# Making the low part of a narrowed weight piece on VectorE instead of GpSimd

## The chip, the core and the metric

The kernel runs on one core of a Trainium2 chip. The metric is device time in microseconds (us), the median of several executions. Five engines work side by side, each through its own instructions in program order: TensorE (PE in the rows, with its weight loads as PEld), VectorE (DVE), ScalarE (ACT), GpSimd (POOL) and SyncE (SP), which here only issues transfers. They wait for one another by semaphores.

## What is computed

Clustered attention, then a mixture of experts with one expert for a token, then a bilinear layer. Only the last two matter here:

```python
def _moe_ref(x, expert_emb, tau, w1, w2):
    ...
    for e in range(E):
        mask = expert_idx == e
        h = np.maximum(x[mask] @ w1[e], 0.0)
        out[mask] = gate_w[mask, None] * (h @ w2[e])

def _moe2_ref(x, w_a, w_b, w_out):
    a = x @ w_a
    b = x @ w_b
    return (a * b @ w_out).astype(np.float32)
```

There are 1536 tokens of 512 features, 8 experts with 1024 hidden features, and 1536 features in the bilinear layer. `w_a`, `w_b` and `w_out` come as 64-bit floats; the other weights as 32-bit ones.

## The kernel before

**Two-part numbers.** TensorE multiplies numbers of a rounded 32-bit type (fp32r). Each operand is therefore held as a high part (the value rounded to that type) and a low part (the value less the high part), and each product is three matmuls: high by high, low by high and high by low.

**Stages.** After attention come 64 expert steps (8 experts of 8 steps, G = 0 to 63) and 72 bilinear steps (I = 0 to 71, G = 64 on). In an expert step, `layer1` makes 12 matmuls of 256 columns; ScalarE takes the high part of the result (`hh`, L944), VectorE the low part (`hl`, L945). `layer2` multiplies what was made two steps before (LAG = 2), with 6 matmuls of 512 columns. In a bilinear step, `bil1` makes 24 matmuls of 256 columns into `ab`; ScalarE copies the first half to `ga` (L1005), VectorE multiplies by the second half (L1006), ScalarE rounds to `gh` (L1009) and VectorE makes `gl` (L1013). `bil2`, two steps later, makes 6 matmuls of 512 columns with `gh` and `gl`. The bank that a step's matmuls write is that of two steps before: TensorE can't start a step until VectorE has read that bank (`hl` or `ga`). At G = 53, G = 61 and I = 1, eight transposes on TensorE and two VectorE instructions of 128x512 (`xTl`, L869) prepare the rows of the next expert or block, and at G = 57 and I = 1 a copy `ys` of 128x512 (L967) is added on VectorE.

**Narrowing.** The 64-bit weights are 36 pieces of 128x512 numbers, 4 in a chunk and 9 chunks. A piece comes by a transfer of 512 KB into one of four `raw` buffers. ScalarE (`narrow_a`, L823) makes `a`, the absolute value taken from the upper words; VectorE (`narrow_b`, L835 to L837) puts in the low bits and the sign, in three instructions, in place. A step later ScalarE (`narrow_c`, L843) copies `a` to the chunk's high part `hi`, and GpSimd (L844) makes the low part, `a` less `hi`. `raw` is free again after L837, `a` (five buffers) after L844. An expert step narrows one piece, from G = 53 on; an even bilinear step one, an odd one two, until the 36 are done at I = 16. The lists `narrowed` and `late` hand pieces from one function to the next; from I = 2 on an even bilinear step finds two pieces in `late`, an odd one one.

**Order.** No scheduler moves instructions: each engine runs what the Python loop writes, in that order. In a bilinear step VectorE has `ga`, the three of one piece, `gl` and, in an odd step, the three of a second piece. In an expert step it has `hl` and then the three of one piece. Chunks 3 and 4 are first read at I = 8, chunks 6 and 7 at I = 16.

Of the kernel before, what the change touches and what calls it, by code (L numbers as in the profile page):

```python
# [44 lines left out]
def kernel(  # L45
# [15 lines left out]
    nc = tc.nc  # L61
# [667 lines left out]
    def result_rows():  # L729

        GA = [P, B * NT, NE]
        GB = B * NT
        tmp = big.tile([P, DM], F32, tag="a", name="rr", bufs=NA)
        t3 = tmp[:, :GB * NE].rearrange("p (t e) -> p t e", e=NE)
        t1, t2, t4, slot_f = (tmp[:, GB * (NE + i):GB * (NE + i + 1)] for i in range(4))
        nc.vector.tensor_copy(slot_f, slot_i)
        for dst, val in ((t1, ebase), (t2, pbase.rearrange("p (o e) -> p o e", o=1)), (t4, obase.rearrange("p (o e) -> p o e", o=1))):
            nc.vector.tensor_tensor(out=t3, in0=oh_all, in1=val.to_broadcast(GA), op=ALU.mult)
            nc.vector.tensor_reduce(out=dst, in_=t3, axis=AX.X, op=ALU.add)

        nc.vector.tensor_sub(slot_f, slot_f, t1)
        nc.vector.tensor_scalar(out=t1, in0=slot_f, scalar1=float(CAP), scalar2=None, op0=ALU.is_ge)
        nc.vector.tensor_sub(t4, t4, t2)
        nc.vector.scalar_tensor_tensor(out=t4, in0=t4, scalar=-float(CAP), in1=t1, op0=ALU.add, op1=ALU.mult)
        nc.vector.tensor_add(t4, t4, t2)
        nc.vector.tensor_add(slot_f, slot_f, t4)
        nc.vector.tensor_copy(slot_i, slot_f)
# [34 lines left out]

    narrowed = []
    late = []

    def open_part():
        n, j = divmod(nsplit[0], 4)
        if j == 0:
            hl[n] = big.tile([P, 2, 4, 512], F32R, tag=f"w{n % NSLOT}", name=f"w_{n}")
        w = raw.pop(nsplit[0])  # L790
        nsplit[0] += 1
        return w, hl[n][:, 0, j, :], hl[n][:, 1, j, :]
# [17 lines left out]
    def split_some(m):  # L810
        for _ in range(m):
            split_hi(1)
            split_lo()
# [3 lines left out]
    def narrow_a(m):  # L817
        for _ in range(min(m, 4 * NCH - nsplit[0])):
            load_raw()
            w, hi, lo = open_part()  # L820
            if w.dtype == I32:
                a = big.tile([P, 512], F32, tag="a", name=f"a_{nsplit[0]}", bufs=NA)
                nc.scalar.activation(a, w[:, :, 1].bitcast(F32), AF.Abs, scale=2.0 ** -112)  # L823
                narrowed.append((w, a, hi, lo))
            else:
                nc.scalar.copy(hi, w)
                nc.gpsimd.tensor_sub(lo, w, hi)
            ndone[0] += 1
            load_raw()

    def narrow_b(m):
        for _ in range(min(m, len(narrowed))):
            w, a, hi, lo = narrowed.pop(0)
            low, top, au = w[:, :, 0].bitcast(U32), w[:, :, 1].bitcast(U32), a.bitcast(U32)
            nc.vector.tensor_scalar(out=au, in0=au, scalar1=3, scalar2=None, op0=ALU.logical_shift_left)  # L835
            nc.vector.scalar_tensor_tensor(out=au, in0=low, scalar=29, in1=au, op0=ALU.logical_shift_right, op1=ALU.bitwise_or)  # L836
            nc.vector.scalar_tensor_tensor(out=au, in0=top, scalar=0x80000000, in1=au, op0=ALU.bitwise_and, op1=ALU.bitwise_or)  # L837
            late.append((a, hi, lo))

    def narrow_c():  # L840
        while late:
            a, hi, lo = late.pop(0)
            nc.scalar.copy(hi, a)  # L843
            nc.gpsimd.tensor_sub(lo, a, hi)  # L844


    xe_t = {}
# [10 lines left out]
    def trans_x(key, src, first=False):  # L858

        hi = big.tile([P, DC, CAP], F32R, tag="xTh", name=f"xTh_{key}", bufs=2)  # L860
        lo = big.tile([P, DC, CAP], F32R, tag="xTl", name=f"xTl_{key}", bufs=2)
        pts = [ps_t.tile([P, 2, CAP], F32, tag=("pp", "pv")[u], name=f"xT_{key}_{u}") for u in range(2)]
        for t in range(CT):
            for j in range(DC):
                nc.tensor.transpose(pts[j // 2][:, j % 2, t * P:(t + 1) * P], src[:, t, j * P:(j + 1) * P], ident)
        for u in range(2):
            (nc.vector.tensor_copy if u and first else nc.scalar.copy)(hi[:, 2 * u:2 * u + 2, :], pts[u])
        for u in range(2):
            nc.vector.tensor_sub(lo[:, 2 * u:2 * u + 2, :], pts[u], hi[:, 2 * u:2 * u + 2, :])  # L869
        xT_t[key] = (hi, lo)  # L870

    def mm3(ps, pairs):

        ops = [o for (sh, sl_), (mh, ml) in pairs for o in ((sh, mh), (sl_, mh))]
        ops += [(sh, ml) for (sh, _), (_, ml) in pairs]
        for i, (s_, m_) in enumerate(ops):
            nc.tensor.matmul(ps, s_, m_, start=(i == 0), stop=(i == len(ops) - 1))  # L877
# [57 lines left out]
    def layer1(G):  # L935
        e, f = divmod(G, NF)
        c, ff = divmod(f, 4)
        w = hl[4 * e + 2 * c]
        xh, xl = xT_t[e]
        ph = ps_t.tile([P, CAP], F32, tag=f"et{G % 2}", name=f"h_{G}")  # L940
        mm3(ph, [((w[:, 0, j, ff * P:(ff + 1) * P], w[:, 1, j, ff * P:(ff + 1) * P]), (xh[:, j, :], xl[:, j, :])) for j in range(DC)])
        hh = big.tile([P, CAP], F32R, tag="hh", name=f"hh_{G}", bufs=4)
        hlo = big.tile([P, CAP], F32R, tag="hl", name=f"hl_{G}", bufs=4)
        nc.scalar.activation(hh, ph, AF.Relu)  # L944
        nc.vector.scalar_tensor_tensor(out=hlo, in0=ph, scalar=0.0, in1=hh, op0=ALU.max, op1=ALU.subtract)  # L945
        hs[G] = (hh, hlo)
# [48 lines left out]
    def bil1(I):  # L995
        ck, f = order[I]
        c, ff = divmod(f, 4)
        xh, xl = xT_t["b", ck]
        pab = ps_t.tile([P, 2, CAP], F32, tag=f"et{I % 2}", name=f"ab_{I}")
        for z in range(2):  # L1000
            w = hl[NCE + 3 * c + z]
            mm3(pab[:, z, :], [((w[:, 0, j, ff * P:(ff + 1) * P], w[:, 1, j, ff * P:(ff + 1) * P]), (xh[:, j, :], xl[:, j, :])) for j in range(DC)])
        narrow_a(PACE[I % len(PACE)] > 0 if I >= I0 else 0)
        ga = big.tile([P, CAP], F32, tag="ga", name=f"ga_{I}", bufs=2)
        nc.scalar.copy(ga, pab[:, 0, :])  # L1005
        nc.vector.tensor_mul(ga, pab[:, 1, :], ga)  # L1006
        gh = big.tile([P, CAP], F32R, tag="hh", name=f"gh_{I}", bufs=4)
        gl = big.tile([P, CAP], F32R, tag="hl", name=f"gl_{I}", bufs=4)
        nc.scalar.copy(gh, ga)  # L1009
        narrow_c()  # L1010
        narrow_a(PACE[I % len(PACE)] > 1 if I >= I0 else 0)
        narrow_b(1)
        nc.vector.tensor_sub(gl, ga, gh)  # L1013
        narrow_b(1)
        gs_[I] = (gh, gl)

    def bil2(I):
# [36 lines left out]
    for G in range(total_f + tot + LAG):  # L1054
        I = G - total_f

        room = 4 * (NSLOT + 2 * (max(G - LAG, 0) // 4)) - nsplit[0]
        if 4 * NCE <= nsplit[0] and I < 0:
            narrow_a(min(room, 1))
        if I < 0:  # L1060
            layer1(G)
            e, f = divmod(G, NF)
            if G == 2 * NF:
                result_rows()
            if G > 3 * NF:
                next(gg, None)
            if f == 5:
                if e + 1 < NE:
                    trans_x(e + 1, xe_t[e + 1])
                else:  # L1070
                    trans_x(("b", 0), x2_t[0])
                if e + 2 < NE:
                    load_xe(e + 2)
                else:
                    load_x2(e + 2 - NE)
        elif I < tot:
            bil1(I)
            ck, f = order[I]
            if I == 1:
                trans_x(("b", 1), x2_t[1])  # L1080
            if I == X2:
                load_x2(2)
                load_x2(3)
            if ck > 0 and f == NF2 - 2 and ck + 1 < NCK:
                trans_x(("b", ck + 1), x2_t[ck + 1])
                if ck + 3 < NCK:
                    load_x2(ck + 3)
        if G - LAG >= total_f:
            bil2(I - LAG)
        elif G >= LAG:  # L1090
            layer2(G - LAG)
        put_rows(G - LAG)
        if nsplit[0] < 4 * NCE:
            split_some(min(room, 2 * G + lead - nsplit[0], RAMP0 + RAMP * G - nsplit[0], 4 * NCE - nsplit[0]))
        elif I < 0:
            narrow_c()
            narrow_b(1)


# [28 lines left out]
```

## Time and profile before

| | |
|---|---|
| median of 3 executions | 836.23 us (835.68 to 838.9) |
| the profiled execution | 841.22 us, its span 839.5 us |
| expert steps | up to 509 us of the span |
| the 36 pieces are narrowed | 478 to 602 us |
| bilinear steps | from 509 us |

The profile is one execution. Its page gives the busy time of every engine over the whole span; the trace behind it can be asked for a stretch, a line, or for instructions in order of time. A time in brackets behind a row is idle time ahead of that instruction, with what ended it. The length given for an instruction overlaps the start of the next one; what an instruction costs in a row of others is the distance from its start to the next start, called its pitch below.

### The profile page before, as it was taken

Reading aid. Unit: us, or ns where it says so; the run is one execution under the profiler, and the core shown is the slowest. Engines: PE = TensorE matmul, PEld = TensorE weight load, DVE = VectorE, ACT = ScalarE, POOL = GpSimd, SP = SyncE. Lnnn points to the kernel's source line nnn. Section 1 sums busy time; section 2 is a strip of 40 time slices with the busy share of each in tenths; the row PEclk is TensorE's granted clock in tenths of the full one; section 3 lists DMA queues with packets and bytes.
Section 4 is the critical chain, followed back from the end, with each engine's and each line's share of the span. In section 5 each row is a group of like instructions: output and inputs, shape, how many; then the busy total and the mean of one; then the engine's idle time right before and its main releaser. Section 6 shows DMA issues by size and latency. Waiting matters only on the chain.

```text
span 839.5 us, 13963 instructions
## 1 busy us (share of the span) xinstructions
PE 794.1 (95%) x5362; PEld 671.9 (80%) x5362; DVE 497.8 (59%) x939; ACT 389.8 (46%) x848; POOL 188.9 (23%) x190
## 2 busy tenths in 40 slices
PE   8889999999999959899999999989999999999996
PEld 5667777677776639789999879878899999999996
DVE  6776676776777667695655499999622221222221
ACT  4555756657556546565555455445322221222211
POOL 5022203134000042232135354444311010010101
PEclk9999999999999979999999999999999999999999
DMA  6137223153120039776777756655010010000000
GB/s 190 39 98 244 57 59 93 40 179 111 29 58 11 1 110 313 266 234 248 250 209 215 194 179 218 213 169 162 14 51 26 9 44 1 1 26 1 27 1 25
DMA packets 45516, 92.63 MB, mean 110 GB/s; under 512 B 6392, under 2 KB 15224, under 8 KB 45440
## 3 DMA queue, kind: packets, MB, share of 16 engines
q1 hardware_dynamic: 41232, 81.67, 32.2%
q0 software_dynamic: 2304, 6.31, 2.0%
q10 hardware_dynamic: 1904, 3.67, 1.3%
q8 instruction: 44, 0.72, 0.4%
q14 instruction: 32, 0.26, 0.1%
HBM read 69.27 MB, written 14.69 MB: 100 GB/s over the span
## 4 chain that ended last, share of the span: by engine, by line
PE 37%; issue 33%; DVE 17%; DMA 6%; POOL 3%; ACT 3%; SPq 0%; POOLq 0%; ACTq 0%; DVEq 0%
PE et L478 7%; PE h L877 6%; PE pv L505 6%; PE y L960 5%; DMA raw<-in_moe_w_dram 5%; PE sc L449 3%; PE sc L450 3%; DVE a L836 3%; DVE nmx L458 2%; PE t L341 2%; DVE a L835 2%; DVE a L837 2%; DVE gl L1013 1%; PE st L366 1%; PE px L519 1%
## 5 line engine op out<-in xcount | busy, mean ns | idle before, releaser
L1006 DVE TENSOR_TENSOR ga<-ab,ga 128x256 f32<-128x256 f32 x72 | 30.4, 422 | 150.4 <-ACT ga L1005 150.4
L463 ACT ACTIVATE E<-sc,nmx 128x768 f32<-128x768 f32 x96 | 86.8, 904 | 64.9 <-DVE nmx L458 57.6
L458 DVE TENSOR_REDUCE nmx<-sc 128x1 f32<-128x768 f32 x96 | 91.6, 955 | 11.0 <-PE sc L450 9.1
L1005 ACT COPY ga<-ab 128x256 f32<-128x256 f32 x72 | 26.6, 370 | 152.9 <-PE ab L877 152.9
L478 PEld LDWEIGHTS et<-ident,E 128*128 128x128 f32 x576 | 63.1, 143 | 34.5 <-issue 12.9
L1032 PE MATMUL o<-w,gh 128*128 128x512 f32 x288 | 90.7, 396 | 0.0
L484 DVE COPY ET<-et 128x384 f32<-128x384 f32 x96 | 52.8, 550 | 62.3 <-PE et L478 62.1
L478 PE MATMUL et<-ident,E 128*128 128x128 f32 x576 | 83.8, 281 | 3.9 <-ACT E L463 3.6
L800 ACT CAST w<-raw 128x512 fp32r<-128x512 f32 x128 | 72.9, 619 | 25.1 <-DMA raw<-in_moe_w_dram 21.5
L806 DVE TENSOR_TENSOR w<-raw,w 128x512 fp32r<-128x512 f32 x96 | 70.5, 762 | 22.6 <-ACT w L800 16.8
L877 PEld LDWEIGHTS h<-xTh,w 128*128 128x128 f32 x512 | 68.8, 190 | 16.3 <-DVE hl L945 11.1
L960 PE MATMUL y<-w,hh 128*128 128x512 f32 x256 | 81.1, 398 | 0.0
L877 PE MATMUL h<-xTh,w 128*128 128x256 f32 x512 | 73.0, 285 | 7.0 <-DVE hl L945 6.2
L505 PE MATMUL pv<-ET,v 128*64 128x384 f32 (+2 forms) x408 | 73.2, 479 | 0.7 <-ACT ET L482 0.6
L449 PE MATMUL sc<-K,Q 80*128 80x512 f32 x192 | 73.2, 382 | 0.4 <-DMA Q<-ohT 0.4
L844 POOL TENSOR_TENSOR w<-a,w 128x512 fp32r<-128x512 f32 x36 | 55.5, 1551 | 72.8 <-ACT w L843 54.4
L806 POOL TENSOR_TENSOR w<-raw,w 128x512 fp32r<-128x512 f32 x32 | 42.9, 1340 | 111.0 <-ACT w L800 96.4
L1009 ACT CAST gh<-ga 128x256 fp32r<-128x256 f32 x72 | 29.2, 406 | 71.9 <-DVE ga L1006 71.9
L450 PE MATMUL sc<-K,Q 128*128 128x512 f32 x192 | 62.1, 344 | 0.0
L1043 POOL DMA_INDIRECT out_dram<-ot,res x12 | 11.7, 972 | 219.9 <-DVE ot L1042 218.6
L1032 PE MATMUL o<-w,gl 128*128 128x512 f32 x144 | 56.6, 393 | 2.3 <-DVE gl L1013 2.3
L1013 DVE TENSOR_TENSOR gl<-ga,gh 128x256 fp32r<-128x256 f32 x72 | 41.4, 574 | 25.9 <-ACT gh L1009 25.9
(268 smaller groups left out, 1595.1 us busy)
## 6 DMA issues: line engine op xcount, KB each, us to landing
raw<-in_moe_w_dram SPq DMA_DIRECT2D x64, 512.0 KB
raw<-in_moe_w_a_dram SPq DMA_DIRECT2D x12, 512.0 KB
raw<-in_moe_w_b_dram SPq DMA_DIRECT2D x12, 512.0 KB
raw<-in_moe_w_out_dram SPq DMA_DIRECT2D x12, 512.0 KB
xs_d<-zero SPq DMA_DIRECT2D x8, 512.0 KB
ys_d<-ys SPq DMA_DIRECT2D x16, 256.0 KB
xe<-xs_d ACTq DMA_DIRECT2D x7, 512.0 KB
v<-in_v_dram SPq DMA_DIRECT2D x8, 384.0 KB
```

Source lines behind the costliest of these rows:

```text
L449: nc.tensor.matmul(ps[:, lo:hi], Q3[:, qs], K3[:, h * S + lo:h * S + hi], start=True, stop=False)
L450: nc.tensor.matmul(ps[:, lo:hi], Q2[:, qs], K2[:, h * S + lo:h * S + hi], start=False, stop=True)
L458: nc.vector.tensor_reduce(out=nmx[pp][:, h, t:t + 1], in_=sc[s], axis=AX.X, op=ALU.max, negate=True)
L463: nc.scalar.activation(e, sc.pop(s), AF.Exp, bias=nmx[pp][:, h, t:t + 1], accum_out=sums[pp][:, t, h:h + 1])
L478: nc.tensor.transpose(pt[:, j * P:(j + 1) * P], e[:, kt * P:(kt + 1) * P], ident)
L505: nc.tensor.matmul(pv[h * D:(h + 1) * D, :], vt[:, h, kt, :], ets[g, h][:, kt, :n * P], start=(kt == 0), stop=(kt == NT - 1))
L800: nc.scalar.copy(hi, w)
L806: eng.tensor_sub(lo, w, hi)
L844: nc.gpsimd.tensor_sub(lo, a, hi)
L877: nc.tensor.matmul(ps, s_, m_, start=(i == 0), stop=(i == len(ops) - 1))
L960: nc.tensor.matmul(ys_ps[e][t], s_[:, t * P:(t + 1) * P], w[:, m_, ff, :], start=(f == 0 and i == 0), stop=(f == NF - 1 and i == 2))
L1032: nc.tensor.matmul(o_ps[ck][t], s_[:, t * P:(t + 1) * P], w_[:, m_], start=(f == 0 and i == 0), stop=(f == NF2 - 1 and j == len(o_f[ck]) - ...
```

## The change

`narrow_c` no longer makes the low part on GpSimd. It puts the piece into a new list `lows`, and a new function `narrow_d` makes the low parts on VectorE. It is called at the end of an expert step, after `narrow_b`, and at the end of `bil1`, after the last `narrow_b`.

```diff
+    lows = []
...
         while late:
             a, hi, lo = late.pop(0)
             nc.scalar.copy(hi, a)
-            nc.gpsimd.tensor_sub(lo, a, hi)
+            lows.append((a, hi, lo))
+
+    def narrow_d():
+        while lows:
+            a, hi, lo = lows.pop(0)
+            nc.vector.tensor_sub(lo, a, hi)
...
         narrow_b(1)
         nc.vector.tensor_sub(gl, ga, gh)
         narrow_b(1)
+        narrow_d()
         gs_[I] = (gh, gl)
...
         elif I < 0:
             narrow_c()
             narrow_b(1)
+            narrow_d()
```

VectorE's instructions before, in expert step G = 56 and at the start of the next: `a_...` is a piece, `hl_...` the low part of the step's result; the number behind a name is the buffer's.

```order
L945 SCALAR_TENSOR_TENSOR hl_6478<-h_6464,hh_6477 128x256
L835 TENSOR_SCALAR a_6460<-a_6460 128x512
L836 SCALAR_TENSOR_TENSOR a_6460<-raw_6345,a_6460 128x512
L837 SCALAR_TENSOR_TENSOR a_6460<-raw_6345,a_6460 128x512
L945 SCALAR_TENSOR_TENSOR hl_6511<-h_6497,hh_6510 128x256
```

The same place in the changed kernel, where later lines have moved down by 1 to 7; `w_...` is a chunk.

```order
L951 SCALAR_TENSOR_TENSOR hl_6478<-h_6464,hh_6477 128x256
L836 TENSOR_SCALAR a_6460<-a_6460 128x512
L837 SCALAR_TENSOR_TENSOR a_6460<-raw_6345,a_6460 128x512
L838 SCALAR_TENSOR_TENSOR a_6460<-raw_6345,a_6460 128x512
L850 TENSOR_TENSOR w_6347<-a_6428,w_6347 128x512
L951 SCALAR_TENSOR_TENSOR hl_6511<-h_6497,hh_6510 128x256
```

One instruction of 128x512 has come in ahead of the next step's `hl`; it works on the piece of the step before.

VectorE's instructions before, in bilinear steps 5 and 6 (an odd one and an even one), from the odd step's `ga` on:

```order
L1006 TENSOR_TENSOR ga_7076<-ab_7047,ga_7076 128x256
L835 TENSOR_SCALAR a_7072<-a_7072 128x512
L836 SCALAR_TENSOR_TENSOR a_7072<-raw_6915,a_7072 128x512
L837 SCALAR_TENSOR_TENSOR a_7072<-raw_6915,a_7072 128x512
L1013 TENSOR_TENSOR gl_7080<-ga_7076,gh_7079 128x256
L835 TENSOR_SCALAR a_7084<-a_7084 128x512
L836 SCALAR_TENSOR_TENSOR a_7084<-raw_6966,a_7084 128x512
L837 SCALAR_TENSOR_TENSOR a_7084<-raw_6966,a_7084 128x512
L1006 TENSOR_TENSOR ga_7131<-ab_7101,ga_7131 128x256
```

The changed kernel from the second piece of that odd step to the start of the next odd step (its buffer numbers differ by one from some row on):

```order
L836 TENSOR_SCALAR a_7083<-a_7083 128x512
L837 SCALAR_TENSOR_TENSOR a_7083<-raw_6966,a_7083 128x512
L838 SCALAR_TENSOR_TENSOR a_7083<-raw_6966,a_7083 128x512
L850 TENSOR_TENSOR w_6975<-a_7019,w_6975 128x512
L1012 TENSOR_TENSOR ga_7131<-ab_7101,ga_7131 128x256
L836 TENSOR_SCALAR a_7127<-a_7127 128x512
L837 SCALAR_TENSOR_TENSOR a_7127<-raw_6978,a_7127 128x512
L838 SCALAR_TENSOR_TENSOR a_7127<-raw_6978,a_7127 128x512
L1019 TENSOR_TENSOR gl_7135<-ga_7131,gh_7134 128x256
L850 TENSOR_TENSOR w_6975<-a_7072,w_6975 128x512
L850 TENSOR_TENSOR w_6975<-a_7083,w_6975 128x512
L1012 TENSOR_TENSOR ga_7182<-ab_7153,ga_7182 128x256
```

An odd step ends with one low part, an even step with two, each ahead of the next step's `ga`. VectorE has 36 instructions more than before, all of this kind. GpSimd has none left between the last rows of the expert weights and the first rows of the output.

## Rows read from the trace of the kernel before

**Rows 1.** The page, part 1: busy us, share of the span, instructions.

```profile
PE 794.1 (95%) x5362; PEld 671.9 (80%) x5362; DVE 497.8 (59%) x939; ACT 389.8 (46%) x848; POOL 188.9 (23%) x190
```

**Rows 2.** Windows: stretch, length, busy us (instructions) of each engine, granted clock, DMA, GB/s.

```profile
479.30:599.80 120.50, 112.32 (x744) 99.00 (x744) 117.21 (x162) 57.72 (x124) 54.19 (x35) 1.00 0.57 174
604.90:820.00 215.10, 215.10 (x1526) 202.43 (x1525) 50.55 (x112) 45.94 (x112) 10.62 (x20) 1.00 0.05 18
```

**Rows 3.** VectorE's groups by line, 479.3 to 599.8 us: count, busy us, mean ns, idle before.

```profile
L837 DVE SCALAR_TENSOR_TENSOR a<-raw,a 128x512 uint32<-128x512 uint32 x36 | 45.9, 1274 | 1.2
L836 DVE SCALAR_TENSOR_TENSOR a<-raw,a 128x512 uint32<-128x512 uint32 x36 | 26.0, 722 | 1.2
L1013 DVE TENSOR_TENSOR gl<-ga,gh 128x256 fp32r<-128x256 f32 x17 | 17.9, 1054 | 0.0
L835 DVE TENSOR_SCALAR a<-a 128x512 uint32<-128x512 uint32 x36 | 17.2, 477 | 0.0
```

**Rows 4.** Timeline (start us, length us) of VectorE and GpSimd, 508 to 512 us.

```profile
508.34 0.69 DVE L837 SCALAR_TENSOR_TENSOR a<-raw,a 128x512 uint32<-128x512 uint32 x1
508.95 0.42 DVE L945 SCALAR_TENSOR_TENSOR hl<-h,hh 128x256 fp32r<-128x256 f32 x1
509.28 0.42 DVE L835 TENSOR_SCALAR a<-a 128x512 uint32<-128x512 uint32 x1
509.73 0.69 DVE L836 SCALAR_TENSOR_TENSOR a<-raw,a 128x512 uint32<-128x512 uint32 x1
509.81 1.77 POOL L844 TENSOR_TENSOR w<-a,w 128x512 fp32r<-128x512 f32 x1 [2.52 <-issue]
510.46 1.67 DVE L837 SCALAR_TENSOR_TENSOR a<-raw,a 128x512 uint32<-128x512 uint32 x1
512.05 0.41 DVE L945 SCALAR_TENSOR_TENSOR hl<-h,hh 128x256 fp32r<-128x256 f32 x1
```

**Rows 5.** Timeline of VectorE: two low parts of expert weights (L806) in a row.

```profile
429.72 1.28 DVE L806 TENSOR_TENSOR w<-raw,w 128x512 fp32r<-128x512 f32 x2
```

**Rows 6.** The page, part 5: all low parts of expert weights on VectorE.

```profile
L806 DVE TENSOR_TENSOR w<-raw,w 128x512 fp32r<-128x512 f32 x96 | 70.5, 762 | 22.6 <-ACT w L800 16.8
```

**Rows 7.** Timeline of TensorE: where steps start, two transposes' rows, one wait.

```profile
479.84 1.21 PE L877 MATMUL h<-xTh,w 128*128 128x256 f32 x8 [0.67 <-DVE hl L945]
...
500.99 0.38 PE L865 MATMUL xT_('b', 0)_0_6663<-ident,x 128*128 128x128 f32 x2
...
501.78 0.71 PE L960 MATMUL y<-w,hh 128*128 128x512 f32 x2
...
503.26 1.12 PE L877 MATMUL h<-xTh,w 128*128 128x256 f32 x8
...
506.08 1.11 PE L877 MATMUL h<-xTh,w 128*128 128x256 f32 x8
...
549.99 0.39 PE L877 MATMUL ab<-xTh_('b', 0)_6661,w 128*128 128x256 f32 x1 [1.17 <-POOL w L844]
...
605.15 1.12 PE L877 MATMUL ab<-xTh_('b', 1)_6850,w 128*128 128x256 f32 x8
...
609.41 1.12 PE L877 MATMUL ab<-xTh_('b', 1)_6850,w 128*128 128x256 f32 x8
```

**Rows 8.** Timeline of VectorE in bilinear steps 5 to 7.

```profile
540.17 0.41 DVE L1006 TENSOR_TENSOR ga<-ab,ga 128x256 f32<-128x256 f32 x1
...
543.39 0.41 DVE L1013 TENSOR_TENSOR gl<-ga,gh 128x256 fp32r<-128x256 f32 x1
...
545.51 0.42 DVE L1006 TENSOR_TENSOR ga<-ab,ga 128x256 f32<-128x256 f32 x1
...
550.14 0.41 DVE L1006 TENSOR_TENSOR ga<-ab,ga 128x256 f32<-128x256 f32 x1
```

**Rows 9.** Timeline of ScalarE in bilinear step 6: the high parts of two pieces.

```profile
546.28 1.14 ACT L843 CAST w<-a 128x512 fp32r<-128x512 f32 x2
```

**Rows 10.** Waits of the queue that issues transfers, 455 to 606 us: total us, times, longest.

```profile
SPq L128 <- DVE a L837: 81.7, 29, 5.0
```

## The prediction

> **What bounds the kernel now.** I read the page first, then the windows of the stretch in which pieces are narrowed, then VectorE's groups there, then the timelines. The page says that TensorE is busy 95% of the span and VectorE 59% [rows 1]; that is a mean over unlike stages. From 479.3 to 599.8 us VectorE is busy 117.21 of 120.50 us and TensorE 112.32, while after 604.9 us TensorE is busy all 215.10 of 215.10 us [rows 2]. So the stretch is VectorE's, and adding anything to VectorE looks like a loss. What matters is what VectorE's time is made of.
>
> It is partly waiting in disguise. L837 takes 0.69 us when GpSimd is idle, and 1.67 us when GpSimd's low part runs beside it: GpSimd started at 509.81 and ended at 511.58, and L837, started at 510.46, ended 0.55 us after that [rows 4]. An undisturbed L837 holds the engine for 0.61 us (508.34 to 508.95), so it did its work behind GpSimd, not beside it. The page of the groups shows how much of this there is: undisturbed, L837 and L836 take 0.69 us, L835 0.42 and `gl` 0.41 [rows 4, 8]. 36 x 0.69 is 24.8 us against 45.9 for L837 and 26.0 for L836; 17 x 0.41 is 7.0 against 17.9 for `gl`; 36 x 0.42 is 15.1 against 17.2 for L835 [rows 3]. The excess is 21.1 + 1.2 + 10.9 + 2.1 = 35.3 us, or 0.98 us a piece. Behind each stretched instruction stands, in VectorE's order, the next `hl`, `ga` or `gl`, for which TensorE waits.
>
> **What TensorE could do.** An expert step without a wait is 503.26 to 506.08, 2.82 us; a bilinear one 605.15 to 609.41, 4.26 us; eight transposes take 500.99 to 501.78, 0.79 us [rows 7]. Between 479.84 and 605.15 lie 9 expert steps (G = 55 to 63), 20 bilinear ones (I = 0 to 19) and two sets of transposes: 9 x 2.82 + 20 x 4.26 + 2 x 0.79 = 112.16 us, while the trace has 125.31. So 13.15 us is the most that any change to VectorE or GpSimd can give here.
>
> **The change, part by part.** Removed: 36 instructions on GpSimd. GpSimd has nothing else in this stretch, so nothing moves up behind them; what goes is the 35.3 us that they put into VectorE's instructions.
>
> Added: 36 low parts on VectorE. The same shape, types and operation stands in L806, where two in a row took 1.28 us [rows 5]; less 0.69 for the last one (an undisturbed L837, of the same size [rows 4]) the pitch is 0.60, rounded up. The mean of all 96 there is 0.762 us, disturbed ones among them [rows 6]. I take 0.60, since GpSimd will be idle; 0.60 and 0.762 are the ends, and an end below nothing is excluded because the instruction occupies VectorE in any case. The sum on VectorE is 36 x 0.60 = 21.6 us more and 35.3 less.
>
> By step, with pitches of 0.33 for `hl`, 0.45 + 0.73 + 0.61 = 1.79 for the three of a piece [rows 4] and 0.33 for `ga` and `gl`, which have `hl`'s length: an expert step on VectorE is 3.10 us now (508.95 to 512.05 [rows 4]) and becomes 0.33 + 1.79 + 0.60 = 2.72, under TensorE's 2.82. Two bilinear steps are 9.97 us now (540.17 to 550.14 [rows 8]). They become 0.33 + 1.79 + 0.33 + 1.20 = 3.65 for the even one and 0.33 + 1.79 + 0.33 + 1.79 + 0.60 = 4.84 for the odd one: 8.49, against TensorE's 8.52. It is close, but VectorE may lag: by the order, TensorE needs `ga` of step I only at the start of step I + 2, which is two `bil2` and one `bil1` later, more than 4.26 us after the matmuls that `ga` reads.
>
> What stays: at G = 53, two `xTl` of (an estimate, from L806's pitch) 0.60 each stand ahead of the first piece, so that step takes VectorE 0.33 + 1.20 + 1.79 = 3.32, 0.5 us over TensorE; at G = 57 the copy `ys`, of that size too, makes 2.72 + 0.60 = 3.32, of which the three shorter steps ahead pay 0.3. I leave 0.8 us for these. `xTl` and `ys` at I = 1 fall into VectorE's lag. The gain is 13.15 - 0.8, about 12.3 us.
>
> The new waits. A low part waits for its high part, at the head of VectorE's queue, with the next `ga` or `hl` behind it. In bilinear step 6 both high parts are done at 547.42 [rows 9], 1.91 us after `ga` began at 545.51 [rows 8]; in the new order the first low part comes up 0.33 + 1.79 + 0.33 = 2.45 us after `ga` began. So it has 0.54 us in hand. Matmuls now wait for low parts of VectorE where they waited for GpSimd: at 549.99 TensorE got the last low part of the second chunk after 1.17 us of waiting [rows 7]. That part was done 549.99 - 545.51 = 4.48 us after `ga` of step 6 began, and will be 3.65 us after it, earlier in the step. `a` is freed with the low part, so no later either. The raw transfers follow VectorE by themselves: SyncE's queue spent 81.7 us waiting for L837, which frees their buffers [rows 10], and ScalarE and the transfers have their old order.
>
> A rule speaks against all this. Perfetto Trace Analysis of the Trainium skill (Optimizing Scalar/DVE Operations) says that with a saturated VectorE it may make sense to give work to ScalarE or even GpSimd; by it the low parts should stay where they are. The same paragraph warns that the two share a port to the memory, and SBUF — State Buffer (SBUF: two separate sides) makes that a lock under which the loser stands still for the whole instruction. The row at 510.46 bears out the second [rows 4]; the first alone would give the sum of the second rival below.
>
> **The rivals.**
> - *VectorE stays the bound.* A low part costs 0.762 and not 0.60, or the lows wait a little. Two bilinear steps are then 8.49 + 3 x 0.16 = 8.97, 0.45 over TensorE, eight times: 3.6 us; an expert step is 2.88, 0.06 over, ten times: 0.6. The gain is 12.3 - 4.2 = 8.1 us at the least. For it: the margin in a pair is only 0.03 us. Against it: L806's pitch, and the lag that is allowed.
> - *The stall isn't GpSimd's.* If something else in the stretch stretched VectorE's instructions, a transfer into the buffers say, the 35.3 us stay and 21.6 us come on top of an engine that has no room: 841.22 + 21.6, slower by 21.6 us. It decides from the point where more than 35.3 - 21.6 = 13.7 us, 0.38 a piece, stays. Against it: the end of L837 follows GpSimd's by 0.55 us, its own work.
> - *Low parts wait for ScalarE.* If the high parts come later by more than the 0.54 us in hand, VectorE's queue stops in every step. Some 27 steps have a low part; at 12.3 / 27 = 0.46 us each, so 1.0 us later, the gain is gone and the time is as before. ScalarE is busy 57.72 of 120.50 us [rows 2], which speaks against it.
> - *The change doesn't do what it says.* The order shows 36 more on VectorE and none left on GpSimd; I give this nothing.
>
> **How the numbers follow.** About 0.5% is what a measurement here tells from no change: 4.2 us. The forecast, a gain of 12.3 us, has 0.65; VectorE as the bound, a gain of 4.2 to 10, 0.22; no change, with ScalarE or a wait that I don't see, 0.07; slower, mostly the stall that isn't GpSimd's, 0.06. Faster is 0.65 + 0.22 = 0.87. The profiled execution would go from 841.22 to 828.9; the median of 836.23 lies 4.99 below that execution, and I take the gain from it: 823.9 us. The low end is all of the 13.15 us and the spread of a median, some 1.2 us on top: 821.9. The high end is the first rival's 836.23 - 8.1 = 828.1 with two of it for more waits: 830.1. The rest, under 0.2, lies above.
>
> **What would show it.** L837 at 0.69 us in all 36 places and `gl` at 0.41; the low part on VectorE at 0.69 with a pitch of 0.60; expert steps of 2.82 and pairs of bilinear steps of 8.5 on TensorE, without waits for `ga`, `gl` or the weights; VectorE busy for some 106 us in the stretch. The prediction is wrong if L837 stays long without GpSimd, if idle time stands ahead of the low parts on VectorE, with ScalarE's copy ending it, or if TensorE's step is above 2.82 or 4.26 with a wait for a raw transfer in front of ScalarE.

## The result, and the profile after

The changed kernel takes 829.85 us (median of four runs, 828.8 to 832.04); the kernel before takes 837.57 us (four runs, 835.68 to 841.27, three of them those that the prediction started from). The ratio is 0.9882, with a 95% interval of 0.9855 to 0.9909: faster by 1.2%. That lies within the stated range (821.9 to 830.1 us), close to its upper end, and 6 us above the forecast of 823.9.

The profiled executions are 841.22 us before and 830.12 after, 11.1 us apart. TensorE's start of step G = 55 and its start of bilinear step I = 20 enclose the stretch that the prediction speaks of. It was 125.31 us long (479.84 to 605.15 [rows 7]) and is now 113.30 (481.07 to 594.37): 12.01 us gained, where 12.3 was forecast. The difference to the 11.1 lies outside the stretch. The stretch begins 1.23 us later, after the same instructions as before (in two further executions of the changed kernel it begins at 478.83 and at 483.03, so this is spread between executions); what follows it is 0.32 us shorter.

The page, part 1 (busy us, share of the span, instructions), answers to [rows 1], and the window below it (length, then busy us and instructions of TensorE, its weight load, VectorE, ScalarE and GpSimd, granted clock, DMA share, GB/s) to [rows 2], both of the changed kernel:

```profile
PE 793.2 (96%) x5362; PEld 675.4 (82%) x5362; DVE 484.2 (58%) x975; ACT 390.9 (47%) x848; POOL 133.3 (16%) x154
```

```profile
479.30:599.80 120.50, 119.61 (x824) 110.66 (x823) 107.03 (x205) 63.34 (x133) 0.00 (x0) 1.00 0.55 176
```

VectorE does 36 instructions more and is busy 13.6 us less over the span. In the window it falls from 117.21 to 107.03 us, while it gets through 205 instructions where it had 162 (in the stretch itself, 481.07 to 594.37, it is busy 105.33 of 113.30 us); GpSimd has none left there; TensorE is busy 119.61 of 120.50 us. The bound has passed from VectorE to TensorE.

VectorE's groups by line in the same window of the changed kernel (count, busy us, mean ns, idle us before) answer to [rows 3]. Later lines have moved down: L837 of before is L838 now, L836 is L837, L835 is L836 and L1013 is L1019; L850 is the low part.

```profile
L837 DVE SCALAR_TENSOR_TENSOR a<-raw,a 128x512 uint32<-128x512 uint32 x36 | 24.9, 693 | 1.2
L838 DVE SCALAR_TENSOR_TENSOR a<-raw,a 128x512 uint32<-128x512 uint32 x36 | 24.9, 692 | 1.2
L850 DVE TENSOR_TENSOR w<-a,w 128x512 fp32r<-128x512 f32 x36 | 24.0, 685 | 0.1
L836 DVE TENSOR_SCALAR a<-a 128x512 uint32<-128x512 uint32 x36 | 15.1, 418 | 0.0
L1019 DVE TENSOR_TENSOR gl<-ga,gh 128x256 fp32r<-128x256 f32 x21 | 8.8, 420 | 1.9 <-ACT gh L1015 1.9
```

Every mean stands at the shortest time that the trace of before showed: L838 at 692 ns (L837 before: 1274), `gl` at 420 (1054), L836 at 418 (477). The low part itself has 685 ns, and only 0.1 us of idle time stands ahead of all 36 of them.

One expert step on VectorE, timeline of the changed kernel (start us, length us), answers to [rows 4]:

```profile
486.79 0.42 DVE L951 SCALAR_TENSOR_TENSOR hl<-h,hh 128x256 fp32r<-128x256 f32 x1
487.12 0.42 DVE L836 TENSOR_SCALAR a<-a 128x512 uint32<-128x512 uint32 x1
487.57 0.69 DVE L837 SCALAR_TENSOR_TENSOR a<-raw,a 128x512 uint32<-128x512 uint32 x1
488.30 0.69 DVE L838 SCALAR_TENSOR_TENSOR a<-raw,a 128x512 uint32<-128x512 uint32 x1
488.91 0.69 DVE L850 TENSOR_TENSOR w<-a,w 128x512 fp32r<-128x512 f32 x1
489.51 0.42 DVE L951 SCALAR_TENSOR_TENSOR hl<-h,hh 128x256 fp32r<-128x256 f32 x1
```

From `hl` to `hl` it is 486.79 to 489.51, 2.72 us, as forecast; the low part has the engine for 0.60 us (488.91 to 489.51). TensorE's starts of steps in the changed kernel answer to [rows 7]:

```profile
481.07 1.22 PE L883 MATMUL h<-xTh,w 128*128 128x256 f32 x8 [0.52 <-DVE hl L951]
...
484.53 1.21 PE L883 MATMUL h<-xTh,w 128*128 128x256 f32 x8 [0.37 <-DVE hl L951]
...
487.45 1.11 PE L883 MATMUL h<-xTh,w 128*128 128x256 f32 x8
...
490.27 1.12 PE L883 MATMUL h<-xTh,w 128*128 128x256 f32 x8
...
543.25 1.12 PE L883 MATMUL ab<-xTh_('b', 0)_6661,w 128*128 128x256 f32 x8
...
547.51 1.12 PE L883 MATMUL ab<-xTh_('b', 0)_6661,w 128*128 128x256 f32 x8
...
594.37 1.12 PE L883 MATMUL ab<-xTh_('b', 1)_6850,w 128*128 128x256 f32 x8
```

Steps are 2.82 us (487.45 to 490.27) and 4.26 (543.25 to 547.51), without the wait for weights of before. The two waits for `hl` at the left edge are what is left. They begin two steps earlier, at G = 53, in rows of ScalarE and VectorE:

```profile
479.63 0.66 ACT L824 ACTIVATE a<-raw 128x512 f32<-128x512 f32 x1 [5.54 <-DMA raw<-in_moe_w_a_dram]
...
480.59 0.42 DVE L951 SCALAR_TENSOR_TENSOR hl<-h,hh 128x256 fp32r<-128x256 f32 x1 [6.30 <-ACT hh L950]
```

ScalarE has the first 64-bit piece ahead of `hh`, and stood 5.54 us for its transfer; so VectorE stood 6.30 us for `hh`, and went into the two `xTl` and the first piece with no time in hand. Its next `hl` came 3.47 us later (484.06), and TensorE's step took 3.46 us. The kernel before has the same wait: 5.69 us on ScalarE, and a step of 3.46 us on TensorE.

On VectorE two bilinear steps take 8.51 us, without idle time between their instructions beyond 0.03 us:

```profile
539.83 0.42 DVE L1012 TENSOR_TENSOR ga<-ab,ga 128x256 f32<-128x256 f32 x1
...
548.34 0.42 DVE L1012 TENSOR_TENSOR ga<-ab,ga 128x256 f32<-128x256 f32 x1
```

### The profile page after: what moved, and what is told of

It is laid out like the page before. It is cut to its first block, busy times and chain, and to the rows that moved or that the text cites. A ratio compares the mean times of both kernels' runs of the same rounds, so it can differ in the third digit from the quotient of the medians.

```text
span 828.4 us, 13922 instructions
## 1 busy us (share of the span) xinstructions
PE 793.2 (96%) x5362; PEld 675.4 (82%) x5362; DVE 484.2 (58%) x975; ACT 390.9 (47%) x848; POOL 133.3 (16%) x154
## 4 chain that ended last, share of the span: by engine, by line
issue 41%; PE 14%; DMA 5%; POOL 1%; ACT 1%; DVE 1%; POOLq 0%; SPq 0%; ACTq 0%
PE h L883 6%; PE y L966 6%; DMA raw<-in_moe_w_dram 3%; POOL out_dram L1050 1%; DMA res<-tab_d 1%; DMA tab_d<-id_gate,slot_i 1%; PE wps L184 1%; DMA ys_d<-ys 1%; PE xT L871 1%; ACT w L801 0%; DVE w L807 0%; POOL w L807 0%; POOLq L1131 0%; DVE hl L951 0%; POOL tick L1055 0%
## 5 line engine op out<-in xcount | busy, mean ns | idle before, releaser
L1039 PEld LDWEIGHTS o<-w,gh 128*128 128x128 f32 x288 | 49.6, 190 | 6.5
L951 DVE SCALAR_TENSOR_TENSOR hl<-h,hh 128x256 fp32r<-128x256 f32 x64 | 26.9, 420 | 41.7 <-ACT hh L950 41.4
```

The lines of the kernel that those rows point to most:

```text
L1039: nc.tensor.matmul(o_ps[ck][t], s_[:, t * P:(t + 1) * P], w_[:, m_], start=(f == 0 and i == 0), stop=(f == NF2 - 1 and j == len(o_f[ck]) - ...
```

## The experiments

Two theories stood against each other. **A**: GpSimd's low part, by running, makes VectorE's instructions stand still; that stall was the bound. **B**: the stall comes from something else, or needs something particular about that instruction. Then there are the place (at the end of a step or at once), the price of a low part on VectorE, and what sets the end now. "The stretch" below is always the time from TensorE's start of G = 55 to that of I = 20.

### The changed kernel again, beside the others

No edit, twice, each time on the same chip as the kernels beside it.

> The changed kernel as it is, for a ratio to the kernel before on the same chip. The sum of the prediction (12.3 us of TensorE's waits gone between the first narrowed piece and bilinear step 20) gives a ratio of 0.985; if part of that is lost elsewhere in a typical run, 0.988 to 0.991. In both cases TensorE's stretch from the wait for the first hl to bilinear step 20 is 113 us and not 125.

Measured: 828.87 us against 840.51, ratio 0.9863 (0.983 to 0.9897); stretch 113.27.

> The changed kernel again, on the chip of the next two, to compare them with. TensorE's stretch from the wait for the first hl to bilinear step 20 is 113 us; ratio to the kernel before 0.985 to 0.989.

Measured: 830.99 us against 841.14, ratio 0.9869 (0.9836 to 0.9902); stretch 113.28. The three stretches of the changed kernel agree within 0.03 us, and 12.0 us of 836 is a ratio of 0.986, which all three intervals contain. The gain is that of the stretch.

### The new place, the old engine

```
     def narrow_d():
         while lows:
             a, hi, lo = lows.pop(0)
-            nc.vector.tensor_sub(lo, a, hi)
+            nc.gpsimd.tensor_sub(lo, a, hi)
```

> The low parts stay on GpSimd, but are issued at the end of the step, where the change has them. Theory (what counts is that GpSimd's instructions stretch VectorE's): GpSimd has nothing else there, its queue is the same, so L837's counterpart stays at 1.6 to 1.8 us in most places, and the time is that of the kernel before, within 2 us. Rival (the new place in the step gives the gain, since weights and buffers come at other moments): the time of the changed kernel, some 10 us less.

Measured: 840.08 us against 840.51, ratio 0.9989 (0.9968 to 1.001); stretch 125.26, as before the change. VectorE's groups in this kernel's stretch:

```profile
L838 DVE SCALAR_TENSOR_TENSOR a<-raw,a 128x512 uint32<-128x512 uint32 x36 | 45.9, 1274 | 1.2
...
L1019 DVE TENSOR_TENSOR gl<-ga,gh 128x256 fp32r<-128x256 f32 x19 | 18.8, 989 | 0.9 <-ACT gh L1015 0.9
```

The long instructions are back, L838 to the nanosecond of [rows 3]. The place alone does nothing; the engine is what counts.

### VectorE, but straight behind the high part

```
             nc.scalar.copy(hi, a)
-            lows.append((a, hi, lo))
+            nc.vector.tensor_sub(lo, a, hi)
```

> The low parts are on VectorE, but right behind the issue of the high part, ahead of narrow_b. Theory (the place behind narrow_b matters, because there the high part is ready): VectorE stands about 0.95 us after each ga, waiting for ScalarE's gh and high part; two bilinear steps take it 10.4 us against TensorE's 8.5, eight times, and expert steps 3.0 against 2.82. Less the lag that is allowed, 12 to 16 us slower than the changed kernel, so 2 to 5 us slower than the one before. Rival (only the engine counts): the time of the changed kernel, within 2 us.

Measured: 847.42 us against 840.51, ratio 1.0078 (1.0049 to 1.0107), 6.9 us slower than before where 2 to 5 were expected; stretch 132.52, so 19.2 us longer than with the low part at the end of the step. The direction was right, the size too small. VectorE's waits in this kernel, 482 to 615 us (what waited, for what, total us, times, longest), and its timeline in a bilinear step:

```profile
DVE w L845 <- ACT w L844: 20.9, 26, 1.0
```

```profile
540.54 0.41 DVE L1012 TENSOR_TENSOR ga<-ab,ga 128x256 f32<-128x256 f32 x1
541.95 1.29 DVE L845 TENSOR_TENSOR w<-a,w 128x512 fp32r<-128x512 f32 x2 [0.99 <-ACT w L844]
```

Between 540.96 and 541.95 VectorE stands with the next work behind it in its queue. It does that 26 times and 20.9 us in all. I had expected that some of this would be absorbed; with VectorE as the bound hardly any was. So the third rival of the prediction, low parts that wait for ScalarE, is a real mechanism with a price above the whole gain, and the place in the change is what keeps it out.

### The stall put back, with the low part where the change has it

After ScalarE's copy, GpSimd makes a second low part into a scratch tile that nobody reads. To make room for it the rings of `hh` and `hl` have three buffers, not four.

```
             nc.scalar.copy(hi, a)
+            junk = big.tile([P, 512], F32R, tag="junk", ...)
+            nc.gpsimd.tensor_sub(junk, a, hi)
             lows.append((a, hi, lo))
```

> The changed kernel, and GpSimd makes each low part as well, at the old moment, into a scratch buffer that nothing reads (two rings of four buffers have three to make room). Theory (GpSimd's instructions, by running, hold VectorE's up): the 35 us of stretching return and the 21.6 us of low parts stay. An expert step on VectorE is 3.7 us against 2.82, ten times, two bilinear steps 11.4 against 8.5, eight times: 25 to 32 us slower than the changed kernel, 15 to 20 slower than before. Rival (the stretching came from waits for GpSimd's results or from something else in the stretch): the time of the changed kernel, VectorE's instructions at 0.69.

Measured: 861.52 us against 840.51, ratio 1.0251 (1.0212 to 1.0291); 32.65 us above the changed kernel beside it and 21.0 above the kernel before, each just over the range expected; stretch 145.12. VectorE's groups in this kernel, 479 to 625 us, and the timelines of GpSimd and VectorE at one piece:

```profile
L852 DVE TENSOR_TENSOR w<-a,w 128x512 fp32r<-128x512 f32 x36 | 32.6, 923 | 0.1
L1021 DVE TENSOR_TENSOR gl<-ga,gh 128x256 fp32r<-128x256 f32 x19 | 26.8, 1411 | 0.9 <-ACT gh L1017 0.9
L838 DVE SCALAR_TENSOR_TENSOR a<-raw,a 128x512 uint32<-128x512 uint32 x36 | 25.9, 719 | 1.2
...
L836 DVE TENSOR_SCALAR a<-a 128x512 uint32<-128x512 uint32 x36 | 23.1, 642 | 0.0
```

```profile
501.03 1.30 POOL L846 TENSOR_TENSOR junk<-a,w 128x512 fp32r<-128x512 f32 x1 [2.53 <-ACT w L844]
```

```profile
501.09 1.52 DVE L836 TENSOR_SCALAR a<-a 128x512 uint32<-128x512 uint32 x1
```

L836 starts 0.06 us behind GpSimd's instruction and ends at 502.61, 0.28 us after that one's end at 502.33. The stretching is spread over other instructions than before, and the sum is nearly the same: over the means of the changed kernel the excess is 32.6 - 24.0 = 8.6 for the low part, 26.8 - 19 x 0.42 = 18.8 for `gl`, 1.0 for L838 and 8.0 for L836, 36.4 us (L837 keeps its 24.9). The prediction read 35.3 us out of the trace of before. The stretch grows by 31.8 of it. This settles it that the stall is GpSimd's: the same instruction there, its result thrown away, brings the stall back whole. SBUF — State Buffer of the Trainium skill (SBUF: two separate sides) describes a lock under which one of the two engines fully blocks; this pair of rows agrees.

### GpSimd as busy, without reading

Three zero fills of the scratch tile stand where the subtraction stood, the first tied to ScalarE's copy, so that they run beside the same VectorE instructions. The rings of `hh` and `hl` have three buffers again.

```
-            nc.scalar.copy(hi, a)
+            c = nc.scalar.copy(hi, a)
+            junk = big.tile([P, 512], F32, tag="junk", ...)
+            for z in range(3):
+                g = nc.gpsimd.memset(junk, 0.0)
+                if z == 0: tc.add_manual_dep(g.ins, c.ins.name, DATA, ...)
```

> The changed kernel, and GpSimd fills a scratch buffer with zeros three times (128x512 each, some 1.4 us in all, an estimate from 0.95 us for a fill of 128x1024 in the trace of before) at the moment at which it made a low part: it is as busy as before, but reads nothing. Theory A (any GpSimd instruction that runs holds VectorE's up): as with the scratch subtraction, 25 to 32 us slower than the changed kernel. Theory B (for VectorE's instructions with two inputs, GpSimd must read as well): the three-operand lines stay at 0.69 us, only the one with a single input (L836) may be longer, by up to 0.5 us: 0 to 8 us slower than the changed kernel.

Measured: 834.79 us against 840.75, ratio 0.9903 (0.9867 to 0.994); stretch 117.92, 4.6 us more than the changed kernel. Groups of GpSimd (478 to 625 us) and of VectorE (483 to 602 us):

```profile
L847 POOL MEMSET junk<- 128x512 f32 x108 | 59.5, 551 | 61.3 <-ACT w L844 56.3
```

```profile
L837 DVE SCALAR_TENSOR_TENSOR a<-raw,a 128x512 uint32<-128x512 uint32 x36 | 24.9, 692 | 1.2
...
L855 DVE TENSOR_TENSOR w<-a,w 128x512 fp32r<-128x512 f32 x36 | 24.0, 684 | 0.1
...
L836 DVE TENSOR_SCALAR a<-a 128x512 uint32<-128x512 uint32 x36 | 22.1, 614 | 0.0
```

GpSimd is busy for 59.5 us, longer than the 54.19 that 35 low parts took before [rows 2], and the two-input instructions of VectorE keep their 692 and 684 ns. Only L836, which has one input, grows from 418 to 614. They did meet: eight fills run in one row from 540.00 to 544.78 (first line), and beside them `gl` and two low parts keep their times, while L836 doesn't.

```profile
540.00 4.78 POOL L847 MEMSET junk<- 128x512 f32 x8
```

```profile
540.03 0.42 DVE L1024 TENSOR_TENSOR gl<-ga,gh 128x256 fp32r<-128x256 f32 x1
540.37 1.29 DVE L855 TENSOR_TENSOR w<-a,w 128x512 fp32r<-128x512 f32 x2
...
541.90 0.65 DVE L836 TENSOR_SCALAR a<-a 128x512 uint32<-128x512 uint32 x1
```

So a busy GpSimd is not enough: the stall of [rows 3] needs something that the subtraction has and a fill has not. Reading is the plain candidate, but the two also differ in their operation, and no run separates that. The same section of SBUF — State Buffer of the Trainium skill says that VectorE's instructions with two inputs in SBUF, the core's own memory, contend only against a GpSimd instruction that reads SBUF, those in a two-port mode against any; both halves agree with these rows, if L836 is of the second kind, which no row here says by itself.

### Half of the low parts on GpSimd

```
-            nc.vector.tensor_sub(lo, a, hi)
+            cnt_d[0] += 1
+            (nc.gpsimd if cnt_d[0] % 2 else nc.vector).tensor_sub(lo, a, hi)
```

> Every second low part on GpSimd, the others on VectorE, all at the end of the step. Theory (a low part on GpSimd costs VectorE 0.98 us by standing still, one on VectorE 0.60 by working): VectorE's 119.7 us become 119.7 - 35.3/2 + 21.6/2 = 113 us, so it stays the bound and some 6.8 us of the 12 are gained: stretch 118 to 120 us, 5 us slower than the changed kernel. Rival (the gain hangs on GpSimd being idle altogether, or on a few places): under 2 or over 10 us gained.

Measured: 832.58 us against 841.14, ratio 0.9915 (0.9876 to 0.9954); stretch 119.08, so 6.2 of the 12.0 us are gained. By the medians the kernel is only 1.6 us slower than the changed one beside it (830.99), where 5 were expected; the stretch, 5.8 us longer, is the surer measure, since executions differ by several us in when it begins. GpSimd's and VectorE's low parts in this kernel, 478 to 625 us, and VectorE's L839, which is L837 of before:

```profile
L852 POOL TENSOR_TENSOR w<-a,w 128x512 fp32r<-128x512 f32 x18 | 26.2, 1456 | 91.5 <-ACT w L845 55.0 <-DVE a L838 21.9 <-issue 11.1
```

```profile
L839 DVE SCALAR_TENSOR_TENSOR a<-raw,a 128x512 uint32<-128x512 uint32 x36 | 31.4, 872 | 1.2
...
L852 DVE TENSOR_TENSOR w<-a,w 128x512 fp32r<-128x512 f32 x18 | 12.3, 682 | 0.1
```

Half of the instructions moved give about half of the gain in the stretch; no other share was tried.

### The low part twice

```
             nc.vector.tensor_sub(lo, a, hi)
+            nc.vector.tensor_sub(lo, a, hi)
```

> The changed kernel with each low part made twice on VectorE. Theory (the changed kernel has VectorE and TensorE level: 8.49 against 8.52 us in two bilinear steps, 2.72 against 2.82 in an expert step): 36 x 0.60 = 21.6 us more on VectorE, of which an expert step shows 0.5, ten times, and two bilinear steps 1.77, eight times: 19 us less the allowed lag, 14 to 19 us slower than the changed kernel. Rival (VectorE has room left after the change): 0 to 5 us slower.

Measured: 850.72 us against 840.75, ratio 1.0091 (1.0062 to 1.012); stretch 135.17, 21.9 us more than the changed kernel. VectorE's timeline in an expert step of this kernel, and TensorE at I = 8:

```profile
487.65 0.68 DVE L850 TENSOR_TENSOR w<-a,w 128x512 fp32r<-128x512 f32 x1
488.37 0.69 DVE L851 TENSOR_TENSOR w<-a,w 128x512 fp32r<-128x512 f32 x1
488.98 0.41 DVE L952 SCALAR_TENSOR_TENSOR hl<-h,hh 128x256 fp32r<-128x256 f32 x1
```

```profile
558.25 0.50 PE L884 MATMUL ab<-xTh_('b', 0)_6668,w 128*128 128x256 f32 x2 [1.16 <-DVE w L851]
```

VectorE has little to spare: 36 instructions more cost TensorE 0.61 us each. I had expected 14 to 19 us. Two things were left out. The second of a pair, which writes the same numbers as the first, starts 0.72 us behind it, not 0.60; and the weights of a chunk come later, so TensorE waits for them at the first step that reads them. The changed kernel sits close to the point where VectorE and TensorE cost the same.

### More of the same kind: the expert low parts too

Ahead of the stretch every fourth expert low part is made on GpSimd. This kernel makes them all on VectorE; it ran twice.

```
-            halves.append((nc.gpsimd if nsplit[0] % 4 == 0 else nc.vector, w, hi, lo))
+            halves.append((nc.vector, w, hi, lo))
```

> The changed kernel, and the 32 low parts of expert weights that GpSimd still makes are on VectorE too. Theory (VectorE's time counts only where it is the bound): in that stretch VectorE is busy 41 of 70 us and TensorE all the time, so 32 x 0.60 = 19 us more and some 7 us less of stretching change nothing, within 2 us of the changed kernel. Rival (GpSimd holds VectorE up wherever both run, and that costs): 3 to 7 us faster.

Measured: 834.02 us against 840.75, ratio 0.9898 (0.9869 to 0.9928).

> The kernel with all expert low parts on VectorE again. In its first profile TensorE waited 4.3 us at 451 to 456 us, before the narrowing, for a low part hl whose high part ScalarE made 9 us late. If that wait belongs to the kernel (GpSimd's twelve table scatters, no longer spaced by its low parts, come in one row there), it is there again and the time is 2 to 6 us over the changed kernel's on the same chip. If it was that execution's alone, the wait is gone and the times are equal within 2 us.

Measured: 832.9 us against 841.14, ratio 0.9896 (0.9855 to 0.9937). This is 1.9 us over the changed kernel beside it, just under the 2 to 6 expected if the wait is the kernel's own. The stretch is 112.34 and 112.32, at the 112.16 that the prediction worked out as TensorE's own. What is gone is ScalarE's wait for the first 64-bit piece: `hl` of G = 53 now comes as promptly as the ones before it. In the first of the two runs:

```profile
482.77 0.43 DVE L951 SCALAR_TENSOR_TENSOR hl<-h,hh 128x256 fp32r<-128x256 f32 x1 [1.02 <-ACT hh L950]
```

The two `xTl` and the copy `ys` stand on VectorE here too, and TensorE waits for nothing in the stretch: they cost nothing where VectorE isn't late. Whether the transfer is in time because of the moved low parts or because of an earlier wait that this kernel has isn't shown. For more is lost before the stretch. TensorE in the two runs:

```profile
455.59 1.40 PE L883 MATMUL h<-xTh,w 128*128 128x256 f32 x8 [4.30 <-DVE hl L951]
```

```profile
449.72 2.07 PE L883 MATMUL h<-xTh,w 128*128 128x256 f32 x8 [4.90 <-DVE hl L951]
```

and ScalarE, whose `hh` that `hl` waits for, in the second of them:

```profile
448.82 0.38 ACT L950 ACTIVATE hh<-h 128x256 fp32r<-128x256 f32 x1 [8.58 <-remote]
```

The wait is in both runs and in none of the three of the changed kernel, so it belongs to this edit. What held ScalarE for 8.58 us the trace does not name; the wait ends 1 to 2 us after the last of twelve table scatters that run in one row on GpSimd. That they are its cause is not shown, and it stays open. The times can't be told from those of the changed kernel, and no version here is faster than that.

## Why the prediction was right, and where it was off

**The mechanism held, step by step.** The reading that VectorE's 117.21 us held some 35 us of waiting rests on comparing an instruction's shortest time with its mean. With GpSimd empty every mean fell to the shortest; with the instruction put back the excess came back as 36.4 us. VectorE's forecast of some 106 us in the stretch came to 105.33, the expert step 2.72 as forecast, the bilinear pair 8.51 against 8.49 forecast and 8.52 on TensorE. The low part costs the lower of its two bounds, 0.60 us.

**The ceiling held.** TensorE's own work was put at 112.16 us, and the stretch came to 113.30; forecast was 0.8 us above that floor, measured 1.14. Of these 0.64 lie in the first step, at whose end TensorE waits 0.37 us for `hl` (the 0.52 us ahead of its start lie outside), 0.1 each in three more expert steps and 0.09 each in the two steps with transposes. So the term was sized 0.3 us too low, the gain 12.3 against 12.0. Its reason was only half right. The step with two `xTl` did take VectorE longer than TensorE (3.47 us, forecast 3.32), but it fell where VectorE was late already, since ScalarE had stood 5.54 us for the first 64-bit piece. In the kernels with all expert low parts on VectorE, where that wait is absent, the same `xTl` and `ys` cost TensorE no wait. The prediction had not counted that wait.

**The step that was off is the last one.** The gain was taken from the median of 836.23, with the profiled execution 4.99 us above it. But the median of the kernel before, in the runs beside each later kernel, was 837.57, 840.51, 840.75 and 841.14: the three runs that I started from lay low, and the profiled execution was the typical one. Its own forecast, 828.9, missed the 830.12 of the profiled execution after by 1.2 us, and that is the later start of the stretch. The range held by 0.25 us, because its upper end had been set by a rival and not by this: that is luck. So the time itself bears the forecast out less well than the stretch does.

**The rivals.** That VectorE stays the bound is refuted for this change (pairs of 8.51 us, no waits), but only just, as the doubled low part shows. That the stall isn't GpSimd's is refuted by the new place alone, which left the stall as it was, and by putting the instruction back. That low parts wait for ScalarE doesn't happen at the end of a step, with 0.1 us of idle ahead of 36 of them, and costs 20.9 us of idle in the earlier place. The time in hand was larger than the 0.54 us forecast: in the changed kernel each low part but the last begins 1.07 us or more after its high part is done. The suggestion of Perfetto Trace Analysis of the Trainium skill (Optimizing Scalar/DVE Operations), that it may make sense to take work off a saturated VectorE, would have had the low parts stay on GpSimd; its own warning on the shared port points the other way, and so do the measured 12 us.

## What to carry to other kernels

A high busy share may hold waiting: set an instruction's shortest time against its mean, and where the mean is far longer, look at what runs on the other engine at that moment. If an instruction on one engine makes another stand still for longer than the other would need to do it itself (here 0.98 us against 0.60), it belongs on the other, even if that one looks full. Put it behind what it needs, not straight after: the same instruction on the same engine, queued at once, lengthened the stretch by 7 us instead of shortening it by 12.

## What the runs showed of the hardware that I had not expected

GpSimd busy for 59.5 us with zero fills left VectorE's two-input instructions at 684 to 692 ns, and stretched only the one-input L836, from 418 to 614 ns; so what a GpSimd instruction costs VectorE depends on both instructions. And two VectorE low parts of 128x512 that write the same numbers follow each other at 0.72 us, where two that write different parts of one chunk follow at 0.60.
